# Squared-ReLU attention with a token mixer, eight batches on one core: one more score block is turned instead of computed, with the buffers and the planning around it

## The chip, the cores and the metric

The kernel runs on one core of one Trainium2 chip. The metric is device microseconds of one execution. TensorE is called PE, VectorE DVE, ScalarE ACT, GpSimd POOL, SyncE SP. PE reads its operands from SBUF and writes PSUM; only DVE and ACT read the score tiles out of PSUM.

## The reference

```python
# batch 8, S = 3200, D = 256, d_qk = d_hyper = 64
scores = (1.0 / S) * np.matmul(z, z.transpose(0, 2, 1))
attn = np.maximum(scores, 0.0) ** 2
x = u * np.matmul(attn, v)
wq, wk = x @ w_q, x @ w_k
W_tok = (1.0 / np.sqrt(64)) * np.einsum('bsd,btd->bst', wq, wk)
mixed = np.einsum('bst,btd->bsd', W_tok, x)
out = np.maximum(mixed, 0.0) @ w_out
```

Since z is multiplied by its own transpose, the scores are symmetric, and so is `attn`. The second half has no nonlinearity between the two token products, so the kernel forms `wk^T x` (64 x 256, the "heads") once for a batch and multiplies `wq` by it.

## The kernel before, in words

The 3200 rows of a batch are 25 tiles of 128. They are also cut into seven groups of columns: six of 512 (groups 0 to 5, four tiles each) and one of 128 (group 6). For each batch and group the kernel needs `attn` of all 25 row tiles against the group's columns, which it multiplies with `v` into four PSUM accumulators (two halves of the group, two halves of the array; `second_product`, L332).

A score tile is one row tile against one group. Two tiles make a pair (`scores`, L247): their matmuls contract over 64 rows only, so one reads z from partitions 0 to 63 and the other from 64 to 127, and they run side by side in the two halves of the array. That is why z^T stands twice in `zT`, once in each half of the partitions. A pair goes into one of two PSUM slots (`ps`), from where DVE (L273) or ACT (L269) takes it through a ReLU into `g`; POOL (L291) or ACT (L289) squares it into a buffer `at`, and PE loads its blocks as weights.

Because `attn` is symmetric, a block of four row tiles against a group need not be computed twice. `is_turned(b, gi, gj)` says for which pairs of groups `gi < gj` the block, made while group `gi` is worked on, is also transposed by a DMA (`turn` in `second_stage`, L311) into a tile `tt`, from which group `gj` takes its weights. Before, these are the groups one and two further on (`FAR = 2`) and the last one, with one exception in batch 0. The tiles of turned blocks come first in a group's order (`near` in the loop that builds `tiles`), `own` are the others.

After a half of a group is complete, `gate` (L348, L349, L370) adds the two accumulators and multiplies by u into x. x is turned by DMA (`turn_x`, L384), projected with both weights (`projections`, L401), copied (L414), the keys turned (`turn_keys`, L419), doubled into both halves by POOL (`double_keys`, L431), and multiplied with x into the heads (`heads`, L438). Heads ride along in the same PSUM slot as the next group's projection (`use_keys`), or in one of their own (`use_heads`, hd). When a batch's heads are known, `mix` (L466) and `proj` (L493) make the output, two batches' work being interleaved.

z of the next batch is loaded by POOL's DMA queue as `zn`, copied by DVE twice side by side into `zd` (`double_z`, L161), and turned by five DMA transposes of five tiles each (`turn_z`, L167). v comes on POOL's DMA queue (`load_v`, L150), u and all transposes and stores go through SP, in order.

The order of all instructions is made by a planner written in the kernel. It keeps a clock for each engine (`give`), takes the next step of PE's work, and puts DMA work into a list with a time from which it may go and a time at which it is due (`move`, `send`, `flush`). `send` books `takes` us on the DMA engines and believes that a transfer has landed `LANDS` us after. The main loop chooses at each step between an extra (keys, mix, proj), a new pair, and a step of the second product; a pair is wanted when its place in the list of all pairs is behind the share of second products done (`lead` = 140 steps ahead). A pair's `at` buffer is one of `NAT`, and it is taken again only when all its rows are used and its turns are planned as landed.

Of the kernel before, what the change touches and what calls it, by code (L numbers as in the profile page):

```python
# [16 lines left out]
def kernel(  # L17
# [10 lines left out]
    nc = tc.nc  # L28
# [23 lines left out]
    NAT = 14  # L52
    NX = 6
# [9 lines left out]
    pxt = ctx.enter_context(tc.tile_pool(name="pxt", bufs=3))  # L63
# [23 lines left out]
    zT, vs, us, xs, xTs, qks, ks, hacc, hss, rts, zds = ({} for _ in range(11))  # L87
# [64 lines left out]
    zdense, ztimes = {}, []  # L152

    def load_z(b):
        zdense[b] = pz.tile([P, NT, dqk], FP16, tag="zn", name="zn")
        nc.gpsimd.dma_start(out=zdense[b][:], in_=rows(z, b))

    def double_z(b, half):
        if half == 0:
            zds[b] = pz.tile([P, NT, 2, dqk], FP16, tag="zd", name="zd")  # L160
        nc.vector.tensor_copy(out=zds[b][:, :, half, :], in_=zdense[b][:])  # L161

    def turn_z(b, i):
        ztimes.append((b, i))
        if i == 0:
            zT[b] = pzt.tile([P, S], FP16, tag="zT2", name="zT2")
# [12 lines left out]
    wq32 = consts.tile([P, NC, dh], FP32, tag="wq32", name="wq32")  # L179
    wk32 = consts.tile([P, NC, dh], FP32, tag="wk32", name="wk32")  # L180
# [59 lines left out]
    made, turned = {}, {}  # L240

    def scores(p):
        assert len(ztimes) >= 5 * tiles[2 * p + 1][0] and p_chunk(p) in z_at, (p, clock, len(ztimes), z_at)
        sc = ps_tile("sc")
        for h, (b, gi, ti) in enumerate(tiles[2 * p : 2 * p + 2]):
            gs, gw = starts[gi], widths[gi]
            nc.tensor.matmul(  # L247
                out=sc[:, h, 0:gw],
                lhsT=zT[b][top(h), ts(ti, P)],
                rhs=zT[b][top(h), ds(gs, gw)],  # L250
                start=True,
                stop=True,
            )
        return sc
# [24 lines left out]
    def second_stage(p, g, ways):  # L279
        at = pat.tile([P, 2 * W], FP16, tag="at", name="at")  # L280
        at0 = 0
        parts = pieces(p)
        if len(ways) > len(parts):
            parts = [(slice(h, h + 1), parts[0][1]) for h in range(2)]
        for (hs, w), on_act in zip(parts, ways * 2):
            n = hs.stop - hs.start
            out = at[:, at0 : at0 + n * w].rearrange("p (n w) -> p n w", w=w)
            if on_act:
                nc.scalar.square(out=out, in_=g[:, hs, 0:w])  # L289
            else:  # L290
                nc.gpsimd.tensor_mul(out=out, in0=g[:, hs, 0:w], in1=g[:, hs, 0:w])  # L291
# [12 lines left out]
        def turn(b, gi, gj, n0, nn, c0, c1):  # L304
            if (b, gi, gj) not in turned:
                kind, nr, bufs = ("l", 1, 8) if gj == LASTG else (gj - gi, 4, gj - gi + 2)
                turned[b, gi, gj] = ptt.tile(
                    [P, nr, 4, P], FP16, tag=f"tt{kind}", name=f"tt{kind}", bufs=bufs
                )
# [32 lines left out]
    def gate(b, gi, half):  # L342
# [9 lines left out]
        if b == last and gi >= LASTG - 2:  # L352
            if gi == LASTG - 2 and half == 0:
                spare = pz.tile([P, NT, 2, dqk], FP16, tag="zd", name="xd")
                spare = spare[:].rearrange("p n a k -> p (n a k)")
                spare = spare[:, 0 : 9 * D].rearrange("p (n d) -> p n d", d=D)
                for i in range(3):
                    xds[LASTG - 2 + i] = spare[:, 4 * i : min(4 * i + 4, 9), :]
# [21 lines left out]
    def turn_x(b, gi):  # L380
        assert len(xTs) < 3
# [192 lines left out]
    LANDS = 4.0  # L574
# [45 lines left out]

    SPLIT = 0.2
# [28 lines left out]
    def squares():  # L650
        while pending and pending[0][0] <= clock[PE] + 0.3:
# [9 lines left out]
            for (b, gi, gj, _, nn, _, _), turn in second_stage(p, g, ways):  # L661
                n = nn * widths[gi] // P
                due = done + (4.0 if gj == gi + 1 else 9.0)
                out_of[p] = out_of.get(p, 0) + 1
                move(done + SLACK, due + SLACK, 1.28, 0.21 * n, turn, lambda t, x=(p, b, gi, gj, nn): block_landed(t, *x))
# [17 lines left out]
    def use_keys(b, gi):  # L683
# [15 lines left out]
        if not final:  # L699
            move(  # L700
                done + SLACK, done + 10.0, 1.28, 0.21 * n, lambda: turn_keys(b, gi),
# [49 lines left out]
    def use_proj(b, gi):  # L751
# [13 lines left out]
        move(done + SLACK, done + 6.0, 0.55, 1.6, stores[0], landed)  # L765
# [5 lines left out]
    Z0 = 24  # L771
    V0 = 56
    V1 = 11

    def batch_begun(b, t):
        if b + 1 < B:
            t0 = max(t + 6, Z0)
            at_time(t0, lambda: (load_z(b + 1), push(3.0)))
            for half in range(2):
                at_time(  # L780
                    t0 + 12 + 3 * half,
                    lambda half=half: (double_z(b + 1, half), give(DVE, clock[PE], 0.98)),
                )
            step = 6 if b else 4
            for i in range(5):
                move(
                    t0 + 18 + step * i, t0 + 34 + step * i, 1.28, 1.05,
# [7 lines left out]
    def v_loaded(b, n0, nn):  # L795
        load_v(b, n0, nn)
        push(2.5)
# [5 lines left out]
    def z_here(p):  # L803
        b = tiles[2 * p + 1][0]
        return not b or z_ready.get((b, 4), 1e9) <= clock[PE]

    def group_begun(b, gi, t):
        if gi == 0:
            batch_begun(b, t)
        if gi + 1 < NG:  # L810
            move(max(t + 2, clock[POOL] + SLACK), t + 7, 0.55, 1.6, lambda: load_u(b, gi + 1))
        elif b + 1 < B:
            move(max(t + 2, clock[POOL] + SLACK), t + 7, 0.55, 1.6, lambda: load_u(b + 1, 0))
# [4 lines left out]
    XWAIT = 3.0  # L818
# [4 lines left out]
    def half_done(b, gi, half):  # L823
# [10 lines left out]
        elif half == halves(gi)[-1]:  # L834
            n = 8 if widths[gi] == W else 2
            move(
                t + SLACK, t + XDUE, 1.28, 0.21 * n, lambda: turn_x(b, gi),
                lambda t: x_landed(t, b, gi), lambda: len(xTs) < 3,
# [55 lines left out]
    def acc_step():  # L894
# [8 lines left out]
        used.add(row)  # L903
        if closes:
# [50 lines left out]
    move(10.0, 14.0, 0.55, 1.6, lambda: load_u(0, 0))  # L955
# [5 lines left out]
    lead = 140  # L961
    turn_about = False
    while groups or work or current["left"]:
# [18 lines left out]
        wanted = able and p * total < (done_acc + lead) * NPAIR  # L982
# [115 lines left out]
```

## Time and profile before

| what | value |
|---|---|
| median of 3 runs | 784.41 us (782.69 to 789.05) |
| the profiled execution | 784.44 us, its span 782.7 us |
| mean granted PE clock | 0.999 |
| busy: PE, POOL, ACT, DVE | 769.8, 645.1, 546.4, 503.3 us |
| score matmuls (512 and 128 columns) | 924 in 462 pairs |
| transposes on SP: tt, ttl, xT, kx, zT | 143, 48, 56, 53, 35 |
| median us from issue to landing: tt, ttl, xT, kx, zT | 4.3, 3.7, 5.8, 4.1, 4.8 |

The span is the time from the first to the last instruction of one execution taken by the profiler. A busy time is the union of an engine's instructions. PE's matmuls are pipelined, so the duration of one (378 ns for a score tile) is longer than the time until the next may start; the place of a matmul in time is best read from starts. PEld is the loading of weights, which overlaps matmuls.

### The profile page before, as it was taken

How to read it: one execution, taken by the hardware profiler on the slowest of the kernel's cores; microseconds unless marked ns; L12 is line 12 of the kernel's file. 1: busy time of each engine (PE TensorE's matmuls, PEld its weight loads, DVE VectorE, ACT ScalarE, POOL GpSimd, SP SyncE). 2: the span in 40 equal slices, each digit the busy share in tenths (PEclk: the TensorE clock that was granted, in tenths of full speed). 3: DMA queues.
4: the chain of work that ended last, by engine and by line, in shares of the span. 5: the costliest groups of instructions: out<-in, count | busy, mean ns of one | idle time of the engine just before them, and what ended most of it. 6: DMA issues, size and time to landing. Idle time of an engine off the chain costs nothing.

```text
span 782.7 us, 28343 instructions
## 1 busy us (share of the span) xinstructions
PE 769.8 (98%) x12410; PEld 663.7 (85%) x12410; DVE 503.3 (64%) x515; ACT 546.4 (70%) x663; POOL 645.1 (82%) x530
## 2 busy tenths in 40 slices
PE   7999999999999999999999999999999999999996
PEld 5899999788899878888889887998889888898784
DVE  6766556655587556786476665777567556566635
ACT  6868777668676767766677767776678676777534
POOL 7898988788889877888789889778788879888961
PEclk9999999999999999999999999999999999999999
DMA  7999999999999999999799989999999998969635
GB/s 179 143 174 170 157 181 180 165 175 206 216 174 177 211 184 189 185 212 189 180 177 174 220 173 201 168 164 217 190 188 152 183 228 166 202 127 210 142 59 213
DMA packets 306300, 140.88 MB, mean 180 GB/s; under 512 B 285056, under 2 KB 287744, under 8 KB 306176
## 3 DMA queue, kind: packets, MB, share of 16 engines
q1 hardware_dynamic: 299408, 122.90, 82.1%
q0 software_dynamic: 6624, 15.98, 15.0%
q8 instruction: 97, 1.59, 0.9%
q10 hardware_dynamic: 144, 0.20, 0.1%
q14 instruction: 27, 0.22, 0.1%
HBM read 59.64 MB, written 26.21 MB: 110 GB/s over the span
## 4 chain that ended last, share of the span: by engine, by line
PE 92%; DVE 2%; DMA 1%; ACT 1%; POOL 1%; issue 1%; DVEq 0%; SPq 0%; ACTq 0%
PE acc L332 67%; PE sc L247 13%; PE fo L493 6%; PE qk L401 3%; PE qk L438 2%; PE mx L466 1%; DVE g L273 1%; DMA v_sb<-in_v_dram 1%; POOL at L291 1%; ACT g L269 1%; ACT at L289 0%; DMA z<-in_z_dram 0%; DVE fo L516 0%; PE hd L438 0%; DVE both L349 0%
## 5 line engine op out<-in xcount | busy, mean ns | idle before, releaser
L291 POOL TENSOR_TENSOR at<-g 128x1024 f16<-128x1024 f32 (+2 forms) x252 | 457.1, 1827 | 62.4 <-DVE g L273 50.3
L332 PE MATMUL acc<-v_sb,at 64*128 64x256 f16 x7344 | 498.4, 269 | 1.2 <-DMA v_sb<-in_v_dram 0.7
L273 DVE TENSOR_SCALAR g<-sc 128x1024 f32<-128x1024 f32 (+2 forms) x320 | 372.6, 1178 | 135.3 <-PE sc L247 126.7
L332 PEld LDWEIGHTS <-at 64*128 64x128 f16 x7344 | 400.9, 94 | 55.2 <-issue 8.1
L289 ACT ACTIVATE at<-g 128x1024 f16<-128x1024 f32 (+2 forms) x230 | 228.1, 1008 | 19.2 <-DVE g L273 17.0
L269 ACT ACTIVATE g<-sc 128x1024 f32<-128x1024 f32 (+2 forms) x159 | 156.5, 986 | 67.1 <-PE sc L247 58.5
L247 PE MATMUL sc<-zT 64*128 64x512 f16 x924 | 187.6, 377 | 1.9 <-DVE g L273 0.8
L370 POOL TENSOR_TENSOR x_sb<-both,u_sb 128x512 f16<-128x512 f32 (+1 forms) x112 | 134.7, 1209 | 43.9 <-DVE both L349 43.6
L332 PE MATMUL acc<-v_sb,tt 64*128 64x256 f16 x2272 | 159.2, 269 | 0.0
L332 PEld LDWEIGHTS <-tt 64*128 64x128 f16 x2272 | 123.5, 94 | 14.3
L349 DVE TENSOR_TENSOR both<-acc,both 128x512 f32<-128x512 f32 (+1 forms) x104 | 69.7, 670 | 86.4 <-ACT both L348 73.3
L348 ACT COPY both<-acc 128x512 f32<-128x512 f32 (+1 forms) x104 | 59.0, 568 | 70.7 <-PE acc L332 66.4
L247 PEld LDWEIGHTS <-zT 64*128 64x128 f16 x924 | 60.8, 94 | 12.9 <-issue 8.9
L521 ACT ACTIVATE fo<-fo 128x1024 f32<-128x1024 f32 (+1 forms) x48 | 44.6, 930 | 24.3 <-PE fo L493 23.8
L493 PE MATMUL fo<-wo,rt 128*128 128x256 f16 x400 | 53.2, 274 | 1.3 <-ACT rt L481 0.5
L483 ACT ACTIVATE rt<-mx 128x1024 f16<-128x1024 f32 (+1 forms) x49 | 45.6, 934 | 11.5 <-PE mx L466 11.2
L414 ACT CAST qk<-qk 128x512 f16<-128x512 f32 (+1 forms) x54 | 29.4, 544 | 30.0 <-PE qk L438 24.1
L493 PEld LDWEIGHTS <-rt 128*128 128x128 f16 x400 | 34.9, 98 | 15.8 <-issue 10.9
L453 DVE TENSOR_TENSOR ha<-qk,ha 128x512 f32<-128x512 f32 x37 | 25.6, 691 | 30.7 <-ACT qk L414 30.2
L401 PE MATMUL qk<-xT_sb,wqk 64*128 64x256 f16 (+1 forms) x404 | 32.4, 265 | 0.0
L431 POOL COPY kx<-kx 128x128 f16<-128x128 f16 (+1 forms) x99 | 26.2, 294 | 5.7 <-DMA kx<-qk 5.7
L438 PE MATMUL qk<-x_sb,kx 64*128 64x256 f16 x342 | 28.4, 269 | 0.0
(45 smaller groups left out, 233.7 us busy)
## 6 DMA issues: line engine op xcount, KB each, us to landing
u_sb<-in_u_dram SPq DMA_DIRECT2D x48, 512.0 KB, 4.9
out_dram<-fo SPq DMA_DIRECT2D x47, 512.0 KB, 5.2
v_sb<-in_v_dram POOLq DMA_DIRECT2D x35, 320.0 KB, 5.5
zn<-in_z_dram POOLq DMA_DIRECT2D x7, 400.0 KB, 6.8
tt<-at SPq DMA_TRANSPOSE x143, 4.3
u_sb<-in_u_dram SPq DMA_DIRECT2D x8, 128.0 KB, 3.1
out_dram<-fo SPq DMA_DIRECT2D x8, 128.0 KB, 3.4
xT_sb<-x_sb SPq DMA_TRANSPOSE x56, 5.8
```

What stands on the lines that cost most here:

```text
L247: nc.tensor.matmul(out=sc[:, h, 0:gw], lhsT=zT[b][top(h), ts(ti, P)], rhs=zT[b][top(h), ds(gs, gw)], start=True, stop=True,)
L269: nc.scalar.activation(out=g[:, hs, 0:w], in_=sc[:, hs, 0:w], func=RELU, scale=GSCALE)
L273: nc.vector.tensor_scalar(out=g[:, hs, 0:w], in0=sc[:, hs, 0:w], scalar1=0.0, scalar2=GSCALE, op0=AOP.max, op1=AOP.mult,)
L289: nc.scalar.square(out=out, in_=g[:, hs, 0:w])
L291: nc.gpsimd.tensor_mul(out=out, in0=g[:, hs, 0:w], in1=g[:, hs, 0:w])
L332: nc.tensor.matmul(out=accs[half, r][:, ds((j % 2) * D, D)], lhsT=weights(b, gi, ti, j)[top(r), :], rhs=vs[b][top(r), ti, :], start=(first ...
L348: nc.scalar.copy(out=both[:, 0 : n * D], in_=accs[half, 0][:, 0 : n * D])
L349: nc.vector.tensor_add(out=both[:, 0 : n * D], in0=accs[half, 1][:, 0 : n * D], in1=both[:, 0 : n * D])
L370: nc.gpsimd.tensor_mul(out=xs[b, gi][:, 0:n, :, r, :].rearrange("p n c d -> p (n c) d"), in0=both[:, 0 : n * D].rearrange("p (m d) -> p m ...
L401: nc.tensor.matmul(out=ps[:, r, 0 : n * P], lhsT=wqk[top(r), c, :, :].rearrange("p t h -> p (t h)"), rhs=xTs[b, gi][top(r), 0:n, c, :], st ...
L483: nc.scalar.activation(out=out, in_=ps[:, 0:nr, 0 : ND * n * P], func=RELU)
L493: nc.tensor.matmul(out=banks[r][:, ds(j * D, D)], lhsT=flat[:, ds((dc * n + j) * P, P)], rhs=wo[:, dc, :], start=(dc == 0 and j == 0), sto ...
```

## The change

Five things change. First, for batches 1 to 7 `is_turned` is also true for groups 0 and 3, so this block is computed once in group 0 and turned, and group 3 takes it from `tt`. Second, z is no longer doubled: `zn` gets a cleared tile at either end and stays dense, and a transpose of two neighbouring tiles (64 + 64 columns) gives tile k-1 in the upper half of the partitions and tile k in the lower. Transposes of the even and of the odd twos go into alternate blocks of a `zT` that is one block longer, so that the upper half's copy of z stands 128 columns further on than the lower's (`z_cols`). It takes four transposes for a batch (7, 7, 6 and 6 blocks). Third, turned blocks other than those of the last group share seven homes of one buffer each, given back when all their rows are used, where before each distance between groups had a ring of its own. Fourth, there are more buffers (`at` 16 for 14, x 7 for 6, xT 4 for 3), found by letting `zd` of batch 0 and the last batch's `xd` use v's buffers and the weights in FP32 use an output buffer. Fifth, the planner's numbers change: landings are believed 8 us after the transfer for 4, a block takes 0.17 us for 0.21, x waits 7 us for 3 before its projection, dues are other, and a pair is wanted by the step at which its group begins (`need`) instead of by its share of all pairs.

```diff
-    NAT = 14
-    NX = 6
+    NAT = 16
+    NX = 7
+    NXT = 4
...
-    zd0 = pz.tile([P, NT, 2, dqk], FP16, tag="zd", name="zd")
+    zd0 = pv.tile([P, NT, 2, dqk], FP16, tag="v_sb", name="zd")
...
-    zT[0] = pzt.tile([P, S], FP16, tag="zT2", name="zT2")
+    zT[0] = pzt.tile([P, S + P], FP16, tag="zT2", name="zT2")
+    zn = pz.tile([P, NT + 2, dqk], FP16, tag="zn", name="zn")
...
+    ZTURNS = [(0, 0, 7), (1, 0, 7), (0, 7, 13), (1, 7, 13)]
     def load_z(b):
-        zdense[b] = pz.tile([P, NT, dqk], FP16, tag="zn", name="zn")
-        nc.gpsimd.dma_start(out=zdense[b][:], in_=rows(z, b))
-
-    def double_z(b, half):
-        if half == 0:
-            zds[b] = pz.tile([P, NT, 2, dqk], FP16, tag="zd", name="zd")
-        nc.vector.tensor_copy(out=zds[b][:, :, half, :], in_=zdense[b][:])
+        nc.gpsimd.dma_start(out=zn[:, 1 : NT + 1, :], in_=rows(z, b))

     def turn_z(b, i):
+        odd, m0, m1 = ZTURNS[i]
...
         nc.sync.dma_start_transpose(
-            out=zT[b][:].rearrange("p (n s) -> p n s", s=P)[:, 5 * i : 5 * i + 5, :],
-            in_=zds[b][:, 5 * i : 5 * i + 5, :, :].rearrange("p n a k -> p (n a k)"),
+            out=zT[b][:].rearrange("p (m o s) -> p o m s", o=2, s=P)[:, odd, m0:m1, :],
+            in_=zn[:, 2 * m0 + odd : 2 * m1 + odd, :].rearrange("p n k -> p (n k)"),
         )
+
+    def z_cols(b, h, at, n):
+        return zT[b][top(h), ds(at + (P if b and h == 0 else 0), n)]
...
     SKIP = [(0, 2)]
+    EXTRA = [(0, 3)]

     def is_turned(b, gi, gj):
         if b == 0 and (gi, gj) in SKIP:
             return False
+        if b and (gi, gj) in EXTRA:
+            return True
...
+    NHOME = 7
+    homes, homes_free = {}, list(range(NHOME))
+
+    def has_home(b, gi, gj):
+        return gj == LASTG or (b, gi, gj) in turned or bool(homes_free)
+
+    def give_home_back(b, gj, t):
+        gi = group_of(t)
+        if (b, gi, gj) in homes and all(
+            (b, gj, starts[gi] // P + n) in used for n in range(widths[gi] // P)
+        ):
+            homes_free.append(homes.pop((b, gi, gj)))
...
-                lhsT=zT[b][top(h), ts(ti, P)],
-                rhs=zT[b][top(h), ds(gs, gw)],
+                lhsT=z_cols(b, h, ti * P, P),
+                rhs=z_cols(b, h, gs, gw),
...
-                kind, nr, bufs = ("l", 1, 8) if gj == LASTG else (gj - gi, 4, gj - gi + 2)
...
+                if gj == LASTG:
+                    tag, nr, bufs = "ttl", 1, 8
+                else:
+                    homes[b, gi, gj] = home = homes_free.pop(0)
+                    tag, nr, bufs = f"tt{home}", 4, 1
...
-    LANDS = 4.0
+    LANDS = 8.0
+    BLOCK = 0.17
+    ROWS4 = 1.3
...
-                due = done + (4.0 if gj == gi + 1 else 9.0)
+                due = done + {1: 4.0, 2: 9.0}.get(gj - gi, FARDUE)
...
+            if b == 0:
+                nc.gpsimd.memset(zn[:, 0 : NT + 2 : NT + 1, :], 0.0)
...
-    XWAIT = 3.0
+    XWAIT = 7.0
...
+    STRETCH = 1.0
...
+        need.append(steps[b, gi] + STRETCH * n * (2 * p - i0) / (i1 - i0))
...
-        wanted = able and p * total < (done_acc + lead) * NPAIR
+        wanted = able and need[p] < done_acc + lead
```

`FARDUE` is 12 us. Other planned times (`ROWS4` 1.3 for 1.6, z's load 2.2 for 3.0, v's 1.8 for 2.5, and `ZWAIT`, `ZDUE`, `ZSTEP`) change in the same manner. `turn_x` allows `NXT` tiles on their way instead of 3.

More of the change, by code (lines that the diff above doesn't have):

```diff
@@ L777, in batch_begun @@
             t0 = max(t + 6, Z0)
[L778 to L785, printed above, removed]
+            if b == 0:
+                nc.gpsimd.memset(zn[:, 0 : NT + 2 : NT + 1, :], 0.0)
+            at_time(t0, lambda: (load_z(b + 1), push(2.2)))
+            step = ZSTEP if b else ZSTEP0
+            for i, (_, m0, m1) in enumerate(ZTURNS):
                 move(
-                    t0 + 18 + step * i, t0 + 34 + step * i, 1.28, 1.05,
+                    t0 + ZWAIT + step * i, t0 + ZDUE + step * i, 1.28, BLOCK * (m1 - m0),
                     lambda i=i: turn_z(b + 1, i),
@@ L961 @@
     lead = 140
+    STRETCH = 1.0
+    need, at, seen = [], 0, 0
+    steps = {}
+    for b in range(B):
+        for gi in range(NG):
+            steps[b, gi] = at
+            at += NT * (widths[gi] // P)
+    first_of = {}
+    for i, (b, gi, t) in enumerate(tiles):
+        first_of.setdefault((b, gi), i)
+    for p in range(NPAIR):
+        b, gi, _ = tiles[2 * p]
+        i0, i1 = first_of[b, gi], ends[b, gi]
+        n = NT * (widths[gi] // P)
+        need.append(steps[b, gi] + STRETCH * n * (2 * p - i0) / (i1 - i0))
     turn_about = False
```

53 lines of the change are left out of this document (29 added, 24 removed).

## The prediction

> **What bounds the kernel now.** I read the page first (busy time, slices, chain), then the busy time by windows, then TensorE's waits, then the groups with their forms, and last the timeline at two places.
>
> The page, its parts 1, 2 and 4:
>
> ```profile
> PE 769.8 (98%) x12410; PEld 663.7 (85%) x12410; DVE 503.3 (64%) x515; ACT 546.4 (70%) x663; POOL 645.1 (82%) x530
> ...
> PE   7999999999999999999999999999999999999996
> ...
> PE 92%; DVE 2%; DMA 1%; ACT 1%; POOL 1%; issue 1%; DVEq 0%; SPq 0%; ACTq 0%
> PE acc L332 67%; PE sc L247 13%; PE fo L493 6%; PE qk L401 3%; PE qk L438 2%; PE mx L466 1%; DVE g L273 1%; DMA v_sb<-in_v_dram 1%; POOL at L291 1%; ACT g L269 1%; ACT at L289 0%; DMA z<-in_z_dram 0%; DVE fo L516 0%; PE hd L438 0%; DVE both
> ```
>
> TensorE is full in every slice but the first and the last, and the chain that ends last is its own matmuls for 92% of the span. No other engine is near that: POOL has 18% to spare, DVE 36%. How much TensorE really stands still, and where, the windows tell (columns: stretch, then busy time of PE, PEld, DVE, ACT, POOL, the granted clock, DMA):
>
> ```profile
> 0.00:25.00 25.00, 20.54 (x264) 15.79 (x266) 16.45 (x22) 16.42 (x27) 19.16 (x25) 1.00 0.79 165
> 25.00:125.00 100.00, 99.25 (x1669) 94.09 (x1665) 64.39 (x65) 78.24 (x94) 90.00 (x74) 1.00 1.11 168
> 125.00:135.00 10.00, 9.99 (x168) 8.96 (x165) 6.58 (x8) 7.48 (x9) 7.97 (x8) 1.00 1.03 189
> 135.00:140.00 5.00, 4.14 (x72) 3.27 (x70) 3.01 (x4) 3.14 (x3) 3.83 (x5) 1.00 0.94 144
> 140.00:760.00 620.00, 619.77 (x10092) 530.40 (x10090) 400.50 (x405) 431.25 (x513) 520.40 (x419) 1.00 0.99 182
> 760.00:783.00 23.00, 16.09 (x168) 11.19 (x163) 12.35 (x16) 9.91 (x19) 3.77 (x4) 0.97 0.49 183
> ```
>
> Idle time of TensorE: 4.46 us in the first 25 us, 0.75 to 125, 0.01 to 135, 0.86 to 140 (one wait), 0.23 in the next 620 us, and 6.9 us at the end. So between 25 and 760 us there are 1.85 us to be won by better planning, and everything else must come from TensorE's own list of work. The 0.86 us is a product of x with the keys (hd, L438) that waited for GpSimd's doubling of the keys; the other waits of the list lie mostly in the first 25 us (columns: total us, times, longest):
>
> ```profile
> PE hd L438 <- POOL kx L431: 0.9, 1, 0.9
> PE sc L247 <- DVE g L273: 0.8, 3, 0.4
> PE sc L247 <- ACT g L269: 0.8, 3, 0.3
> PE acc L332 <- DMA v_sb<-in_v_dram: 0.7, 1, 0.7
> ```
>
> **The change, part by part.**
>
> *The new turned block.* In batches 1 to 7 the block (0, 3) is computed once and turned for group 3, where before group 3 computed its own four row tiles. In TensorE's order this shows as 896 score matmuls for 924: 28 fewer, 14 pairs, two in each of seven batches. The second product keeps its 10,000 matmuls; 224 of them take their weights from a turned block instead of `at`, and a load from either takes 94 ns.
>
> ```profile
> L332 PEld LDWEIGHTS <-at 64*128 64x128 f16 x7344 | 400.9, 94 | 55.2 <-issue 8.1 <-POOL at L291 0.4 <-ACT at L289 0.2
> L247 PE MATMUL sc<-zT 64*128 64x512 f16 x916 | 187.6, 378 | 1.9 <-DVE g L273 0.8 <-ACT g L269 0.8
> L332 PEld LDWEIGHTS <-tt 64*128 64x128 f16 x2272 | 123.5, 94 | 14.3
> L161 DVE COPY zd<-zn 128x1600 f16<-128x1600 f16 x14 | 13.7, 975 | 0.0
> ```
>
> The 378 ns of a score matmul is not its price: the two of a pair use different halves of the array and start 4 ns apart. In the chain line L247 has 12.7% of 782.7 us over 462 pairs, 0.215 us for one; in the timeline the next matmul starts 0.21 us after a pair. So 14 pairs are **3.0 us**, all of it on the path, because TensorE is what ends last. This is the one certain term.
>
> *What leaves the other engines.* The 14 pairs also need 14 fewer evictions and squares. By the built order DVE has 308 large evictions for 299, ACT 123 for 146; ACT 220 large squares for 208, POOL 208 for 234; and the 14 doubling copies of z go. With the durations of the groups: POOL 26 x 1.895 = 49 us less, ACT 23 x 1.025 - 12 x 1.055 = 11 us less, DVE 13.7 - 9 x 1.221 = 3 us less. None of it is on the path: these engines already stand idle for 18% and more while TensorE never waits. I count it at nothing; the cover is that spare time. The one cleared buffer row (a memset of 128 x 2 x 64 on POOL, ahead of the first squares) stands in POOL's idle time before 7 us.
>
> *Transposes on SP.* The new blocks add 14 transposes of eight 128x128 blocks, z needs 28 for 35 (182 blocks for 175). So SP issues 7 more transposes, 7 x 1.27 us (median issue in the trace) = 9 us in 783, and the DMA engines carry 119 blocks more on about 2,100. That lies beside TensorE as long as landings stay ahead of use. In the trace a turned block lands 4.3 us after issue, 10.6 at worst, and, laying landings against the first weight load that reads them, 6.3 us or more before its use (median 26); keys have least, 3.4 us. In the new order the distance in TensorE work from the last score pair of a block to its first use is not shorter: in the middle of the run 31 us or more at the lower end against 30, median 48 against 42. I price it at nothing, with the third rival as its bound.
>
> The trace's z turns, contiguous on both sides, land after 4.8 us (median), 8.0 at worst. The Trainium skill (DMA: Bandwidth & Descriptors, Latency and other measured facts) says a transpose with a non-contiguous middle dimension moves 261 GB/s instead of some 350 to 400. The new turn writes every second block and so falls under it; an estimate by that page is 0.9 us instead of about 0.6 for 224 KB, a landing later by some 0.3 us. No row here shows a strided one. By either the sum is the same, since z is finished long before the batch that reads it.
>
> *More buffers, shared homes, later planned landings, pairs by need.* These change the order in which instructions stand, not their number. In stream order the places where a PSUM slot is asked for sooner than its eviction can be done number 23 for 30, about as deep. The first 736 rows of TensorE's order (to about 25 us) are the same, and so are the last 255 (the last 11 us). So the idle time at both ends stays. The single wait at 138 us may go or come back at another of the 53 key turns; bounds 0 and -0.9 us, I take -0.5. In the rest a gain is bounded by the idle time, -1.0, a loss by the depth of the remaining deficits, +1.0; I take 0.
>
> *One place that gets worse.* Near the end, before, the last projection with its heads stood ahead of 28 matmuls on `ttl`, which covered its eviction:
>
> ```profile
> 759.47 0.60 PE L401 MATMUL qk<-xT_sb,wqk 64*128 64x256 f16 x8
> 759.90 0.60 PE L438 MATMUL qk<-x_sb,kx 64*128 64x256 f16 x8
> 760.34 1.69 PE L332 MATMUL acc<-v_sb,ttl 64*128 64x256 f16 x28
> 761.87 0.60 PE L438 MATMUL hd<-x_sb,kx 64*128 64x256 f16 x8
> 762.31 0.38 PE L466 MATMUL mx<-qk,hs 64*128 64x256 f16 x4
> ```
>
> In the new order all 48 `ttl` matmuls stand first, then the projection (16 matmuls), then hd (8), then mx, and mx needs the PSUM slot of the projection two places before. From the last `ttl` step: projection done at 0.87; ACT, behind the last gate copy, casts from 1.08 to 1.67 (0.59 a cast); DVE adds from 1.72 to 2.41 (0.69); mx can start at 2.45, and without the wait would start at 0.87 + 0.44 = 1.31. That is **+1.1 us**, with everything behind it on TensorE. If the eviction is picked up earlier it is 0.
>
> *Sum.* The profiled execution took 784.44 us with a span of 782.7; the median of the runs is 784.41, so what is taken from the span is taken from the median. 784.4 - 3.0 - 0.5 + 1.1 = **782.0 us**.
>
> **The rivals.**
>
> 1. *Planning wins too.* All 1.85 us of idle time between 25 and 760 us goes and the wait at the end does not come: 784.4 - 3.0 - 1.85 = 779.6. For: more slack at most uses of turned blocks, fewer squares on POOL. Against: the waits are few and scattered, and a new order makes new ones. Going below 776.6 would need 3 us more out of the first 25 or the last 23 us, where the order is the same.
> 2. *The pairs were not worth their time, or the change does not tell.* TensorE meets a new wait wherever a pair is gone, and the end costs its 1.1 us: 784.4 + 1.1 = 785.5. Against: the engines that would make it wait also have less to do.
> 3. *SP late (the slower side).* SP issues in order. The two added transposes of each of seven batches fall where z, u, x and four or more other blocks are due as well, and a home that is still being read holds SP; behind it stand the xT and kx turns and the u loads. One transpose's issue takes 1.27 us as a rule, but 5.13 in the worst case of the trace. One such issue ahead of the keys with the least margin is 5.13 - 3.4 = 1.7 us for TensorE; seven of them 12 us: 784.4 - 2.4 + 12 = 794. It beats the gain from 2.4 / 7 = 0.35 us a batch beyond the margin. For: the DMA share is 1.11 in the stretch to 125 us and 0.99 later. Against: the margins of all other transfers are 6 us and more.
>
> **How the numbers follow.** Forecast as summed, 779.5 to 784: 0.52. Rival 1, 776.6 to 779.5: 0.09, and further down 0.07. Rival 2 and its like, 784 to 792.3: 0.19. Rival 3, above 792.3: 0.13. A measurement of this kernel tells about 1% from no change (776.6 and 792.3). Faster by more: 0.07; within: 0.52 + 0.09 + 0.19 = 0.80; slower by more: 0.13. The range runs from rival 1 with 2 us for the scatter of a median (the three runs lie 6.4 us apart) to the middle of rival 2's stretch: 777.5 to 789, leaving about 0.2 outside. The forecast's own range is 779.5 to 784.
>
> **What would show it.** Right: 896 score matmuls and still 98% PE; PE idle under 3 us between 25 and 760 us; PE's busy time near 767; near the end a wait of mx for DVE of about 1.1 us; POOL's busy time near 596. Wrong: TensorE waits for kx, xT or tt landings in several batches, or for evictions in the first group of each batch (rivals 3 and 2), or a score pair that costs other than 0.215 us with z read at two offsets.

## The result, and the profile after

The changed kernel took 796.78 us in the median (five runs, 790.63 to 801.71), the kernel before 784.41. The ratio is 1.0151, interval 1.0116 to 1.0186: slower by 1.5%, where 782.0 us had been forecast. In a later session, with ten runs of its own, the same kernel came to 1.0069 (1.0031 to 1.0108). So it is slower by 0.7 to 1.5%. All ratios below are against the kernel before on the same chip in the same session. As one kernel moved by 0.8% between two sessions, a difference of that size between runs of different sessions is not taken as shown below.

The profiled execution took 790.63 us with a span of 788.8, 6.1 us more than before. It is the quickest of the five, so it shows the least of the loss. The page, parts 1 and 4:

```profile
PE 766.7 (97%) x12382; PEld 660.5 (84%) x12382; DVE 498.1 (63%) x510; ACT 536.4 (68%) x652; POOL 597.6 (76%) x505
...
PE 85%; POOL 4%; DMA 3%; ACT 3%; issue 3%; DVE 2%; SPq 0%; DVEq 0%; ACTq 0%; POOLq 0%
```

PE's busy time is 3.1 us shorter, where the sum had 3.0. But the chain that ends last is PE's matmuls for 85% instead of 92%, and the rest of it is other engines and DMA. Idle time is 788.8 - 766.7 = 22.1 us against 12.9, 9.2 more, and 9.2 - 3.1 is the 6.1 us. Where it lies (columns as in the windows of before: stretch, busy PE, PEld, DVE, ACT, POOL, clock, DMA share, GB/s):

```profile
140.00:300.00 160.00, 154.23 (x2472) 129.67 (x2469) 97.53 (x100) 107.47 (x129) 118.28 (x100) 0.99 1.07 193
...
760.00:789.00 29.00, 20.26 (x236) 14.56 (x233) 14.66 (x19) 11.56 (x22) 5.64 (x5) 0.96 0.44 164
```

From 25 to 760 us PE stands idle for 8.93 us where it was 1.84, and 5.77 of it are between 140 and 300, a stretch that had no idle time before. PE's waits name most of it (total us, times, longest):

```profile
PE fo L511 <- ACT fo L539: 4.3, 1, 4.3
PE hd L456 <- POOL kx L449: 1.6, 2, 0.8
...
PE mx L484 <- DVE ha L471: 1.0, 1, 1.0
```

The last line is the wait near the end that the prediction priced at 1.1 us. The first is new: the output projection waits for ACT's copy out of PSUM into `fo`. Why ACT is late is seen in ACT's timeline (start, duration, and in brackets the idle time before and its releaser) and in SP's queue at that place:

```profile
266.40 1.02 ACT L539 ACTIVATE fo<-fo 128x1024 f32<-128x1024 f32 x1 [5.43 <-DMA out_dram<-fo]
```

```profile
257.08 1.45 SPq L437 DMA_TRANSPOSE kx<-qk  x1
258.63 4.37 SPq L331 DMA_TRANSPOSE ttl<-at  x1
263.10 1.00 SPq L540 DMA_DIRECT2D out_dram<-fo  x2
```

SP issues without a pause here, and the `ttl` turn at 258.63 takes 4.37 us to issue where the one at 266.59 takes 1.22. Behind it stands the store of an older `fo`, which lands 3.2 us after its own issue. There are two `fo` buffers; ACT cannot refill one before its store has landed, so it stands still for 5.43 us, the PSUM slot is not emptied, and PE stands still behind that. POOL, too, stands 6.18 us for a key turn. One more thing stands in this trace: by its landing times nothing of SP's queue landed between 256.20 and 263.45, and the load of u issued at 254.75 took 8.71 us to land (median 5.2); the slow issue at 258.63 ends just before that. Pauses of 6 us and more between SP's landings are in the trace of the kernel before too (four, the longest 6.54 us), and no PE wait of over 0.9 us followed there. So a full queue and a late landing met here, and the trace does not tell what share each has. And the wait costs more than its 4.26 us, as the granted clock shows (column PEclk, the third from the end):

```profile
263.00:267.00 4.00, 0.22 (x5) 0.10 (x1) 0.00 (x0) 0.60 (x1) 2.24 (x3) 1.00 1.10 360
267.00:270.00 3.00, 2.52 (x18) 1.51 (x19) 0.47 (x1) 1.73 (x3) 2.46 (x4) 0.67 0.75 119
270.00:275.00 5.00, 5.00 (x81) 4.48 (x77) 2.96 (x6) 1.82 (x4) 3.24 (x3) 0.86 1.03 323
```

The lost clock is 3 x 0.33 + 5 x 0.14 = 1.7 us. The other four executions have mean clocks of 0.994 to 0.989, the slowest time with the lowest; from 0.997 to 0.989 is 0.008 x 790 = 6.3 of the 11.1 us between the quickest and the slowest.

The transposes land later than before (median us to landing last; before 4.3, 4.1, 3.7):

```profile
tt<-at SPq DMA_TRANSPOSE x157, 4.5
...
kx<-qk SPq DMA_TRANSPOSE x53, 4.6
ttl<-at SPq DMA_TRANSPOSE x48, 4.3
```

POOL doubles the keys, and how long it waits for them is a sign of SP's lateness that can be compared over runs, one profiled execution each (total us, times, longest; in this order the kernel before, the change, and two kernels of the next section: the added block with the planner's numbers of before, and the new numbers without the block):

```profile
POOL kx L431 <- DMA kx<-qk: 5.7, 4, 2.0
POOL kx L449 <- DMA kx<-qk: 34.5, 15, 6.2
POOL kx L449 <- DMA kx<-qk: 1.0, 2, 0.7
POOL kx L449 <- DMA kx<-qk: 28.0, 10, 5.9
```

In these executions the block alone makes hardly a key late, and the new numbers do so without the block.

### The profile page after: what moved, and what is told of

Read it like the earlier page. It is cut to its first block, busy times and chain, and to the rows that moved or that the text cites. A ratio compares the mean times of both kernels' runs of the same rounds, so it can differ in the third digit from the quotient of the medians.

```text
span 788.8 us, 28275 instructions
## 1 busy us (share of the span) xinstructions
PE 766.7 (97%) x12382; PEld 660.5 (84%) x12382; DVE 498.1 (63%) x510; ACT 536.4 (68%) x652; POOL 597.6 (76%) x505
## 4 chain that ended last, share of the span: by engine, by line
PE 85%; POOL 4%; DMA 3%; ACT 3%; issue 3%; DVE 2%; SPq 0%; DVEq 0%; ACTq 0%; POOLq 0%
PE acc L352 61%; PE sc L265 12%; PE fo L511 6%; PE qk L419 3%; POOL at L309 2%; PE qk L456 2%; DMA out_dram<-fo 2%; PE mx L484 1%; DMA v_sb<-in_v_dram 1%; ACT g L287 1%; DVE g L291 1%; POOL x_sb L388 1%; ACT at L307 1%; ACT fo L539 0%; SPq L331 0%
## 5 line engine op out<-in xcount | busy, mean ns | idle before, releaser
L352 PE MATMUL acc<-v_sb,at 64*128 64x256 f16 x7120 | 478.9, 269 | 1.1 <-DVE both L369 0.6
L291 DVE TENSOR_SCALAR g<-sc 128x1024 f32<-128x1024 f32 (+1 forms) x329 | 381.4, 1179 | 138.2 <-PE sc L265 119.0
L309 POOL TENSOR_TENSOR at<-g 128x1024 f16<-128x1024 f32 (+2 forms) x226 | 408.4, 1819 | 59.2 <-DVE g L291 53.0
L352 PEld LDWEIGHTS <-at 64*128 64x128 f16 x7120 | 383.3, 94 | 54.9 <-issue 6.1
L307 ACT ACTIVATE at<-g 128x1024 f16<-128x1024 f32 (+2 forms) x242 | 240.3, 1010 | 28.9 <-DVE g L291 26.4
L265 PE MATMUL sc<-zT 64*128 64x512 f16 x896 | 184.2, 376 | 2.8 <-DVE g L291 1.0
L352 PE MATMUL acc<-v_sb,tt 64*128 64x256 f16 x2496 | 169.9, 270 | 0.0
L287 ACT ACTIVATE g<-sc 128x1024 f32<-128x1024 f32 (+1 forms) x136 | 132.9, 980 | 43.1 <-PE sc L265 37.9
L352 PEld LDWEIGHTS <-tt 64*128 64x128 f16 x2496 | 136.6, 94 | 14.6 <-issue 0.4
L265 PEld LDWEIGHTS <-zT 64*128 64x128 f16 x896 | 58.7, 94 | 12.9 <-issue 9.0
L539 ACT ACTIVATE fo<-fo 128x1024 f32<-128x1024 f32 (+1 forms) x48 | 44.3, 930 | 31.7 <-PE fo L511 23.0
L449 POOL COPY kx<-kx 128x128 f16<-128x128 f16 (+1 forms) x99 | 25.9, 289 | 34.5 <-DMA kx<-qk 34.5
L432 ACT CAST qk<-qk 128x512 f16<-128x512 f32 (+1 forms) x54 | 29.4, 544 | 30.6 <-PE qk L456 27.4
L419 PE MATMUL qk<-xT_sb,wqk 64*128 64x256 f16 (+1 forms) x404 | 32.9, 265 | 0.0
```

The lines of the kernel that those rows point to most:

```text
L265: nc.tensor.matmul(out=sc[:, h, 0:gw], lhsT=z_cols(b, h, ti * P, P), rhs=z_cols(b, h, gs, gw), start=True, stop=True,)
L287: nc.scalar.activation(out=g[:, hs, 0:w], in_=sc[:, hs, 0:w], func=RELU, scale=GSCALE)
L291: nc.vector.tensor_scalar(out=g[:, hs, 0:w], in0=sc[:, hs, 0:w], scalar1=0.0, scalar2=GSCALE, op0=AOP.max, op1=AOP.mult,)
L352: nc.tensor.matmul(out=accs[half, r][:, ds((j % 2) * D, D)], lhsT=weights(b, gi, ti, j)[top(r), :], rhs=vs[b][top(r), ti, :], start=(first ...
L419: nc.tensor.matmul(out=ps[:, r, 0 : n * P], lhsT=wqk[top(r), c, :, :].rearrange("p t h -> p (t h)"), rhs=xTs[b, gi][top(r), 0:n, c, :], st ...
```

## The experiments

Three explanations stood against each other: the added block's turns cost time on SP and the DMA engines; the planner's new numbers cost it, whatever is turned; or the new z, buffers and homes do.

### Which part costs: the block, the numbers, the rest

*The changed kernel without the added block.*

```diff
-    EXTRA = [(0, 3)]
+    EXTRA = []
```

> The changed kernel without the new turned block: group 3 computes its four tiles against group 0's rows itself again (14 pairs more, 3 us of TensorE). Theory A (prices too low): SP is still behind, 790 us or more, waits for fo and kx still there. Theory B (the added transposes): the waits go and 784 to 786 us are left. Theory C: 790 or more.

Measured: 791.37 us, ratio 1.0070 (1.0034 to 1.0105). The profiled execution is its quickest, 784.68 us; it shows no wait of PE over 1.3 us behind the start, and a span of 782.9, so where the other executions lose their time is not seen. Against this kernel the block of the change (1.0151 and 1.0069) costs between nothing and 0.8% net, by the session.

*The layout alone, with the planner of before.* z by overlapping twos, buffers and homes as changed; no added block; prices, landings, dues, `XWAIT` and the rule for pairs of before.

```diff
-    EXTRA = [(0, 3)]
-    LANDS = 8.0
-    BLOCK = 0.17
-    ROWS4 = 1.3
+    EXTRA = []
+    LANDS = 4.0
+    BLOCK = 0.21
+    ROWS4 = 1.6
...
-        wanted = able and need[p] < done_acc + lead
+        wanted = able and p * total < (done_acc + lead) * NPAIR
```

> The changed kernel's z by overlapping twos, its buffers and shared homes, without the new block, and with the planner's numbers of before (prices, landings 4, dues, 3 us before a projection, pairs by share). Theory B and its companion E (the planner's numbers are what costs e2 its 5 us, the layout parts are neutral): 782 to 788, as the kernel before. If the turn of z by overlapping twos or the shared homes cost time themselves: over 789.

Measured: 785.44 us, 1.0010 (0.9975 to 1.0044), no difference from before. So of z, buffers and homes together neither gain nor loss is seen. The profiled execution is the slowest of the ten, 793.38 us, and has two long waits of PE for keys, 3.5 and 2.6 us: such waits come now and then without the block and the new numbers too. The 0.6% of the kernel without the block would then be the numbers of the planner; the two runs are of different sessions and their intervals overlap a little, so this is likely, not shown.

*The same with the added block* (`EXTRA = [(0, 3)]`).

> The same with the new block: the block alone on the planner of before. Theory B (the transfers do not fit): 5 us or more slower than e9, 790 to 815. If the new planner's numbers were the whole cost: 3 us faster than e9, 780 to 784.

Measured: 794.73 us, 1.0124 (1.0101 to 1.0147). On the same chip the block turns 1.0010 into 1.0124: 9 us lost net, with 3.0 us of PE work gone, so 12 us gross. But the expectation's reason, transfers that do not fit, is not what the trace shows: hardly a transfer is late (POOL waits 1.0 us for keys, PE 0.9 us for v), and PE waits in many small portions for PSUM slots, most of all:

```profile
PE sc L265 <- DVE g L291: 4.2, 8, 1.2
```

*Another block* (`EXTRA = [(2, 5)]`, the changed kernel otherwise).

> The changed kernel with the block (2, 5) turned in batches 1 to 7 instead of (0, 3): the same 14 pairs saved, the same 14 transposes, but due later in the batch. Theory B in its narrow form (the jam is made in group 0 of a batch): below e2, 786 to 791. Theory B in its wide form (SP is full from 10 to 70 us of every batch, wherever the transfers are put): 793 to 800.

Measured: 802.57 us, 1.0228 (1.0154 to 1.0303), with `PE mx L484` and `PE qk L419` behind ACT's `fo` for 8.1 and 7.1 us. So the loss is not tied to the place of this one block.

*Pairs by share, as before* (only the `wanted` line).

> The changed kernel with pairs wanted by their share of all pairs as before, instead of by need; all else as changed. Theory B: pairs are made earlier or later by some us, and the jam on SP stays: 793 to 802. If the new rule of wanting pairs makes the jam (pairs early in a batch, and their transposes with them): below 790.

Measured: 798.02 us, 1.0182 (1.0142 to 1.0222). Taking the new rule for pairs back does not remove the loss.

### The planner's two numbers

The change lowers the price of a turned block (`BLOCK`, with `ROWS4` and the loads) and lengthens the time in which a transfer is believed to land (`LANDS`). Each was taken back or made alone, in three kernels.

*The changed kernel with the old prices* (`BLOCK` 0.21, `ROWS4` 1.6, loads 3.0 and 2.5):

> The changed kernel with the planner's old prices of DMA work (0.21 us a block for 0.17, 1.6 us for four rows of u or out for 1.3, z's load 3.0 for 2.2, v's 2.5 for 1.8); everything else as changed. Theory A (the new prices are too low: the planner sends more to SP and the DMA engines than they take, SP falls behind its plan, and output stores and keys land late for TensorE): the long waits of TensorE for ACT fo and POOL kx go, 780 to 784 us. Theory B (the added transposes of the new block are themselves too much for SP in the first half of a batch): still 790 or more, with kx and fo waits as in the changed kernel. Theory C (the late landings and waits in the plan, 8 and 7 us, bunch the extras): still 790 or more.

Measured: 816.77 us, 1.0403 (1.0362 to 1.0445).

*The changed kernel with* `LANDS = 4.0`:

> The changed kernel with a landing believed 4 us after the transfer, as before the change, instead of 8. Theory C (late planning makes the waits): 782 to 786 us. Theories A and B (SP runs behind its plan and the 8 us are what hides a part of it): slower still, over 800 us.

Measured: 822.55 us, 1.0453 (1.0388 to 1.0519).

*The old prices without the block* (`EXTRA = []`, prices as above):

> The changed kernel without the new block and with the planner's old prices of DMA work. Theory B with true old prices (without the block the plan fits into what SP can send, and the prices of before describe it): 782 to 787 us, below e2's 791.4. If the old prices hurt by themselves, as e1 (816.8 with the block) would have it: over 795.

Measured: 813.82 us, 1.0350 (1.0289 to 1.0410).

*The kernel before with the new prices*, and *the kernel before with* `LANDS = 8.0`:

> The kernel before with nothing but the new, lower prices of DMA work in its planner (0.17 us a block, 1.3 us for four rows, 0.85 for a z turn, 2.2 and 1.8 us for z and v). Theory A: slower than before by 5 us or more, with new waits of TensorE for kx, tt or fo. Theories B and C: as before, within 3 us of 784.

> The kernel before with a landing believed 8 us after its transfer instead of 4, nothing else. e1 and e6 (old prices with 8 us) took 814 to 817 with little scatter. If it is the pair of old prices and 8 us that stalls the plan itself: 800 to 820, many small waits of TensorE for DVE g and none for kx or fo. If it was something else in the changed planner: 783 to 789.

Measured: 792.40 us, 1.0104 (1.0052 to 1.0156), and 803.17 us, 1.0236 (1.0215 to 1.0256).

| ratio to before | high price, short landing | low price, long landing | high, long | low, short |
|---|---|---|---|---|
| kernel before | 1 | not run | 1.0236 | 1.0104 |
| new layout, no block | 1.0010 | 1.0070 | 1.0350 | not run |
| new layout and block | 1.0124 | 1.0151 and 1.0069 (the change) | 1.0403 | 1.0453 |

(The column of high price and short landing has the other numbers of before as well in its last two rows.) The two numbers make up for each other, in most part, and each without the other costs 1.0 to 3.4% more than the first column, far more than the whole forecast gain of 0.3%. The two sides lose in different ways. First the changed kernel with the old prices, then with the short landing:

```profile
PE sc L265 <- DVE g L291: 11.6, 16, 1.2
```

```profile
PE qk L456 <- POOL kx L449: 15.2, 7, 4.5
PE mx L484 <- ACT fo L539: 8.5, 3, 6.4
```

Where the planner books much, no key and no store is late (POOL and ACT wait for none), the four runs lie within 0.7 us, and PE waits 16 times for some 0.7 us at the score pairs. Where it books little, keys and stores land late (POOL waits 63.9 us for keys), PE waits ten times for them, 2.4 us on average and at most 6.4, once 2.7 us for xT, and the four runs scatter over 15 us. That the plan itself runs dry in the first case is argued from this form, not measured.

### Is it the transfers themselves?

*Spare turns.* The kernel without the block, and with 14 transposes of eight blocks each, booked like the others, into a tile that nothing reads (one home fewer to make room).

```diff
-    NHOME = 7
+    NHOME = 6
...
+                move(done + SLACK, done + FARDUE + SLACK, 1.28, BLOCK * 8, lambda p=p: turn_spare(p), lambda t, p=p: spare_landed(t, p))
...
+        nc.sync.dma_start_transpose(out=spare[:], in_=made[tiles[2 * p]][0][:])
```

> The changed kernel without the new turned block, but with 14 transposes of eight blocks from the same place in group 0 of batches 1 to 7 into a tile that nobody reads: the transfers of the new block, and none of its matmuls saved. In the second e2 (no block, no transfers) took 791.4 us. Theory B (SP and the DMA engines have no room for these transfers in the first two thirds of a batch): 6 us or more over e2, 797 to 803, with waits of TensorE for kx or fo of the kind seen in the changed kernel. Theory D (not the transfers, but the use of the new block or the lost pairs make the waits): as e2, 789 to 793.

Measured: 804.42 us, 1.0248 (1.0173 to 1.0323), against 1.0070 without them in another session. PE's waits in the slowest of the four, which was profiled:

```profile
PE qk L456 <- POOL kx L449: 9.1, 3, 5.0
PE sc L265 <- ACT fo L539: 5.5, 1, 5.5
```

*The same with one block in each spare transpose* (still booked as eight, so the order is the same).

```diff
-        nc.sync.dma_start_transpose(out=spare[:], in_=made[tiles[2 * p]][0][:])
+        nc.sync.dma_start_transpose(out=spare[:, 0:1, :], in_=made[tiles[2 * p]][0][:, 0:P])
```

> e5 with each of its 14 spare transposes cut to one 128x128 block out of eight; every other instruction in the same place as in e5, so SP's queue has the same number of issues. If places in SP's queue cost (14 x 1.27 us of issue): as e5, 800 to 808. If the data cost: as e2, 788 to 794.

Measured: 802.59 us, 1.0188 (1.0114 to 1.0262). With an eighth of the data most of the loss is still there; the intervals overlap, and the two runs are of different sessions, so what the data cost is not shown. The rest could be the 14 issues, or the other order that the planner makes when it has booked them.

*Spare turns without a booking.* The kernel without the block, 14 transposes of eight blocks put into SP's queue, unknown to the planner; room for them from one x buffer and one of the pool `pq`. In the traces PE, DVE, ACT and POOL have the order of the run without the block, instruction for instruction.

```diff
-    NX = 7
+    NX = 6
...
+        if spare_todo and spare_todo[0][0] <= clock[PE]:
+            turn_spare(spare_todo.pop(0)[1])
```

> The changed kernel without its added turned block, with 14 transposes of eight 128x128 blocks that nothing reads issued from SP, and without any booking of them by the planner: the order of the instructions of PE, ACT, DVE and POOL stays that of the run without the added block, all but a few lines (in the run with booked spares it was another order). Theory A (SP has no room for them: issue and transfer cost by themselves): stores or keys late, ratio to the kernel before 1.015 to 1.03, with waits of PE of 3 to 7 us behind ACT's copies into fo or POOL's of kx. Theory B (the planner's new order after the bookings cost the time, the transfers lie beside other work): as the run without the added block, ratio 1.00 to 1.01, and no wait of PE over 2 us that that run does not have.

Measured: 794.28 us, 1.0133 (1.0086 to 1.0180), between what the two theories expected. Against 1.0070 the transfers by themselves cost some 5 us, and the order after booking, with one home fewer, the other 9 of the 14 us. Both are estimates across sessions, and in the first the intervals overlap a little. The two buffers taken away are not a likely cause: the kernel with three `fo` buffers below lacks the same two and is quicker. POOL waits 52.9 us for keys here. The longest wait (SP, then POOL, then PE):

```profile
242.31 13.38 SPq L331 DMA_TRANSPOSE tt<-at  x4
255.78 2.08 SPq L437 DMA_TRANSPOSE kx<-qk  x1
```

```profile
259.15 0.52 POOL L449 COPY kx<-kx 128x128 f16<-128x128 f16 x2 [9.21 <-DMA kx<-qk]
259.63 3.74 POOL L309 TENSOR_TENSOR at<-g 128x1024 f16<-128x1024 f32 x2
```

```profile
261.58 1.03 PE L352 MATMUL acc<-v_sb,at 64*128 64x256 f16 x8 [4.17 <-POOL at L309]
```

Four transposes occupy SP for 13.38 us; the keys' turn is behind them; POOL, in order, stands 9.21 us before the copy of the keys, and the squares behind that copy are what PE then waits for. It is the same lateness by another way. No spare turn stands near: the last one before was issued at 199.33. That it still tells 60 us later is argued from SP's rows, which have no pause of over 0.5 us from there to 279.5; without the spare turns the stretch at this place ends at 268.9.

### Is it the stores' place behind the transposes?

*Stores issued by ACT* (`nc.scalar` for `nc.sync` in the output projection).

> The changed kernel with the output stores issued by ACT instead of SP, so that a store no longer stands behind transposes. If the long waits of TensorE for ACT fo come from stores held on SP: these waits go, 788 to 794 us, and the waits for kx stay. If the stores are late because the DMA engines are late: no change, 795 to 800.

Measured: 802.39 us, 1.0164 (1.0075 to 1.0252). The profiled execution is the slowest of the four (811.49 us). In it PE waits for ACT's casts of the projections (`PE sc L265 <- ACT qk L432`, 6.4 us in three) and evictions of scores (5.4 in four), with the stores now in ACT's order, and for `fo` (4.1 in two). Taking the stores off SP alone gains nothing.

*A quarter of each store*, in the changed kernel and in the kernel before, and beside them *the changed kernel once more*.

```diff
-                out=rows(out, b)[:, n0 + at : n0 + at + n, :],
+                out=rows(out, b)[:, n0 + at : n0 + at + 1, :],
```

> The changed kernel storing one of the four row tiles of each output group (three quarters of the output are left out), same instructions in the same order: 20 MB of 145 less for the DMA engines. If the data jam the transfers: the waits for fo and most for kx go, 779 to 788 us. If places in SP's queue do it: 792 to 798.

> The control: the kernel before with the same quarter of its output stored. It has 1.85 us of waits inside its run and a last store to end with: 780 to 785 us by every theory; if the changed kernel is freed by less data, e14 comes out below this one by up to 3 us, the 14 pairs.

> The changed kernel once more, unaltered, for a second trace: 790 to 802 us. By the reading so far the added time is in waits of TensorE for ACT fo (whose buffer waits for a store) and for POOL kx (which waits for a landing), in whichever batches the jam is worst, and in matmuls after such waits under a lower granted clock.

Measured: 790.01 us, 1.0037 (1.0002 to 1.0071); 783.58 us, 0.9984 (0.9951 to 1.0016); 790.26 us, 1.0069 (1.0031 to 1.0108). With 18.7 MB of 26.2 fewer to write, the changed kernel lands between what the two theories expected, its interval overlaps that with all of them, and the control shows no gain: the bytes of the stores are at most a small part of the loss. The long wait is still there in the profiled execution, the slowest of the ten: `PE mx L484 <- ACT fo L539: 7.9, 1, 7.9`. There the store was not issued late, it landed late: issued at 458.29, it landed after 9.0 us (median of the stores 3.2), behind a `ttl` turn that was issued at 456.90 and landed after 10.0. So a store can be late in both ways, by its place in SP's queue, as in the first profile, or by transfers ahead of it that do not land.

*Three buffers for* `fo` (one x buffer and one buffer of the pool `pq` fewer, where the expectation names xT; the order on every engine is that of the changed kernel).

```diff
-            fo = pg.tile([P, 2, W], FP32, tag="fo", name="fo", bufs=2)
+            fo = pg.tile([P, 2, W], FP32, tag="fo", name="fo", bufs=3)
```

> The changed kernel with three fo buffers for two, the room for it taken from elsewhere (one xT buffer and one pq buffer fewer); the order on every engine as in the changed kernel. If the loss is carried by stores that stand late behind transposes on SP, so that ACT cannot refill fo and PE's PSUM slot is not freed: the waits of PE on ACT's copies into fo go (some 5 us of 790), ratio to the kernel before 0.998 to 1.004. If SP's lateness finds another way (keys, xT, the next store): ratio 1.007 to 1.015 as the changed kernel has it, with waits on POOL's kx or on xT in their place.

Measured: 788.65 us, 1.0018 (0.9981 to 1.0055), the best of the kernels with the block, and as fast as the kernel before within the uncertainty. Yet the wait that it was to take away is there in the profiled execution, one copy further on:

```profile
PE sc L265 <- ACT fo L539: 5.0, 1, 5.0
```

```profile
251.95 7.22 SPq L331 DMA_TRANSPOSE tt<-at  x3
...
264.35 1.00 SPq L540 DMA_DIRECT2D out_dram<-fo  x2
```

```profile
270.00:273.00 3.00, 3.00 (x29) 2.93 (x30) 0.91 (x3) 0.58 (x1) 3.00 (x4) 0.50 0.89 155
273.00:280.00 7.00, 7.00 (x98) 6.81 (x95) 4.66 (x6) 3.99 (x7) 4.08 (x5) 0.79 1.14 281
```

Its interval overlaps that of the unaltered changed kernel (1.0069), so that the third buffer helps is likely, not shown. PE's waits for keys shrink to 0.4 us, POOL's do not (37.9 us). No version of the changed kernel beats the kernel before.

## Why the prediction was wrong

*Right.* The one term that it called certain: PE's busy time fell by 3.1 us (3.0 forecast; that the sizes agree so well is in part luck, since the 1.7 us of lost clock lie within it and something else must have become shorter, which stays open), score matmuls are 896, POOL's busy time 597.6 us (596). The wait of mx near the end came with 1.0 us (1.1). Changing z to overlapping twos, sharing homes and more buffers cost nothing together, as forecast: 1.0010. On z the Trainium skill (DMA: Bandwidth & Descriptors, Latency and other measured facts), which gives a transpose with a non-contiguous middle dimension less bandwidth, would by the prediction's estimate have had it land some 0.3 us later; the trace has 4.9 us for six or seven strided blocks against 4.8 for five contiguous ones, which is no sign of it, though medians with other transfers in the queue could hide 0.3 us.

*The step that failed: "Transposes on SP", priced at nothing.* The runs showed a cost in its place: with the planner of before the block lost 9 us net, on one chip and clear of the noise; with the new numbers it lost between nothing and 0.8%, by the session, and the profile of the change has a store that lands late, with 4.3 us of PE's time and 1.7 us of clock behind it. How the turns cost this is in part argued: with the planner of before the loss came through the order of the plan, with waits at PSUM slots, and only with the new numbers through late transfers. Three things in the step's working were wrong.

First the size. Seven more issues at the median 1.27 us made 9 us. In the traces SP's transposes took 548.7 us in all before and 579.9 after (335 and 342 issues, summed from their rows): 31 us, not all of it from the added turns, since the order changed too. The median is not the mean: 68 issues before and 83 after took over 2 us, 186 and 231 us together. That sum, and not the count, had to be set against the room.

Second the room. 9 us "in 783" is an average. By the rows of SP's issues, cut in stretches of 10 us from the start of a batch on (6 us ahead of its load of the next z) and averaged over five batches, SP is busy for 93 to 95% of the time from 10 to 70 us of each batch in the kernel before, and for 56 to 91% in the rest, slow issues included. The added turns come from the first group of each batch; in the changed kernel the first 10 us went from 68 to 90%, the last from 65 to 90%. The margin of the keys, 3.4 us at the least before, was gone after: POOL waited for them 15 times for 34.5 us in all, where it had been four times and 5.7.

Third the path. Margins were taken for what PE reads: keys, xT, `tt`. The transfer that held PE longest was one that nothing reads, the store. It frees `fo`; `fo` frees ACT, ACT the PSUM slot. The prediction named only xT, kx and u as what stands behind the transposes in SP's queue. Rival 3, "SP late", at a chance of 0.13, comes nearest to what the profiles of the change show. That its 794 us are near the measured time is luck: it had the keys as the only way to PE, and a like toll in each batch, where the two profiled executions of the changed kernel have one wait over 2 us each, behind a store, and a lower clock after it; and it blamed the turns, where the new numbers made keys late without them (28.0 us).

*The second step that failed: the planner's numbers, 0 with 1 us to either side.* This was bounded by PSUM slots counted in the built order, with every transfer taken to land as planned. Either of the two without the other cost 1.0 to 3.4%. Both together, without the block, likely cost some 0.6%, 5 us. Each of these runs has another order of instructions, with waits of its own; a change of the planner's prices had to have bounds of its own.

*The gain of 0.5 us at 138 us* did not come; waits for `kx` grew from 0.9 to 1.6 us.

Open: why the same kernel is 0.7% slower in one session and 1.5% in another; whether SP's full queue or the late landings ahead of it weigh more; how the 9 us of the booked spare turns divide between the order and the one home fewer; and whether three `fo` buffers truly gain.

## What to carry to other kernels

Work that is moved from a full engine to an in-order queue is priced by the queue's room in the stretch where it lands, with issue times summed, not by the median issue and the average share. In that queue, follow the transfers that nothing reads as well: a store is a buffer's release, and the buffer's writer, and what that writer frees, wait for it. Where a planner has a price and a landing time for transfers, each may have been tuned against the other: here either one changed alone cost more than the work saved.

## What the runs showed of the hardware

A long wait of PE costs more than its length. In the traces of all these runs, behind the first 20 us and before the end, each of the 21 waits of 3.2 us or more was followed by a lower granted clock, worth 1.4 to 3.1 us in the next 15 us. Shorter ones differ: a wait of 2.56 us (the layout alone) left the clock at 1.00, others of 2.0, 2.4 and 3.0 us were followed by a loss of 1.7. After 4.26 us the granted clock was 0.67 over 3 us and 0.86 over 5, that is half speed for 3.4 us; after 5.0 us (three `fo` buffers) 0.50 over 3 us and 0.79 over 7, half speed for 5.9 us. The 0.86 us wait of the kernel before and a wait of 1.3 us in the kernel without the block left it at 1.00. The Trainium skill (TensorE: Matmul & The Clock Gate, Part 1: The HAM clock gate) says that the array falls to half its clock after an idle window of some 3.4 us and comes back after as long a busy one; these traces agree, the second with a longer return, and with no sharp bound between 2 and 3.2 us.

The issue of a transpose is not a fixed cost. Its median was 1.2 to 1.4 us for one to eight blocks in the changed kernel, its longest 6.7 us. With 14 spare turns SP's transposes took 570.6 us in all where each moved one block of 128x128 (booked) and 576.1 where each moved eight (not booked), against 541.9 without them; these are single executions, the first with another order, and two of the changed kernel differ by 4.4 us. So the number of blocks in a turn told little here.
